# Order and queues of the first loads in a fused attention and feed-forward kernel

## The chip, the cores and the metric

The kernel runs on one core of a Trainium2 chip. The metric is the device time of one launch in microseconds (us). TensorE (PE) does the matmuls and the transposes, VectorE (DVE) and ScalarE (ACT) copy results out of PSUM and do the elementwise work, GpSimd (POOL) issues the loads that change float32 into bfloat16, and SyncE (SP) issues transfers that keep the type.

## What is computed

Attention inside blocks of 64 tokens, and a feed-forward layer with a product of two projections, without a nonlinearity:

```python
scores = scale * np.matmul(q_c, k_c.transpose(0, 1, 2, 4, 3))   # 8 batches, 8 heads, 9 blocks of 64, depth 64
scores = scores - np.max(scores, axis=-1, keepdims=True)
attn = np.exp(scores)
attn = attn / (np.sum(attn, axis=-1, keepdims=True) + 1e-09)
out = np.matmul(attn, v_c)
# heads side by side: x is 4608 x 512
a = x @ w1                 # 512 x 1024
b = x @ w2                 # 512 x 1024
h = a * b @ w3             # 1024 x 1024
return (h @ w_out)         # 1024 x 512
```

## The kernel before

The 4608 tokens are 36 groups of 128 (two blocks of 64 each) for the attention, and 9 tiles of four groups for the feed-forward layer. Since nothing stands between `w3` and `w_out`, the kernel multiplies them once, `w3o = w3 @ w_out`, and a tile then costs two projections (`add_tile`, line 491), one product on VectorE (line 500) and one matmul with `w3o` (line 522).

A group (`add_group`) takes q and k as bfloat16 from a `raw` buffer, of which there are six. Groups 0 to 11 are transposed on TensorE (line 337, with the identity `ident`), later ones by transfers of SyncE (line 341). Then come copies of k and of q's two halves, the scores (line 365), maximum, difference, exponential, sum and scaling, the transposes of the attention (line 396, or line 347 by transfer from group 16 on), the product with v (line 407) and a copy into `xt` (line 411). v is kept for one batch at a time in one of three buffers `vd0` to `vd2`, which are zeroed at the start: the first by VectorE, the other two by ScalarE (line 244). The loads of a batch of v are two transfers, one for each half of the partitions (line 273). Group 4 is the first that needs the second batch of v.

`w3o` is made in eight steps (`add_w3o`): a block of `w3` is transposed with `ident` (line 448), copied, and multiplied with `w_out` in two parts (line 459): with blocks 0 to 3 of `w_out` and with blocks 4 to 7. Blocks 4 to 7 come by one load of GpSimd (`load_wo`, line 301). Blocks 0 to 3 come in float32 by four transfers of SyncE (`stage_wo`, lines 306 to 321) into buffers of `o_sb`, and ScalarE casts them to bfloat16.

The order on every engine is written by a planner, `Plan.run`, which walks through the work with costs and keys, puts each operation on an engine, and emits them in the order in which it started them. What it assumes of transfers decides the order of the program and nothing else; on the chip the engines wait on semaphores. GpSimd's order is given: `LOADS` (lines 18 to 21) is the order of its first loads, with `('ident',)` where it makes the identity (`make_identity`, a memset and a select). `('w3', 7, 8)` is block 7 of `w3`, `('qk', 2)` q and k of group 2 (one transfer each, or two each where the group lies in two batches, as group 4 does), `('v', 0, 0, 2)` the first batch of v, `('w12', 0, 2)` four transfers with the first two eighths of `w1` and `w2`, `('wo', 4, 8)` blocks 4 to 7 of `w_out`. GpSimd's transfers use eight semaphores in turn, so that each issue waits for the landing of the transfer eight before it (`RING = 8`, line 67). `issue` is the time for which the planner thinks the issuing engine busy.

Ahead of the first attention product the kernel also puts fillers on TensorE (lines 575 to 585): matmuls of zeros, 14 at the start and then as many as fit into each gap that the planner sees.

Of the kernel before, what the change touches and what calls it, by code (L numbers as in the profile page):

```python
# [14 lines left out]

LOADS = [('qk', 0), ('w3', 7, 8), ('w3', 3, 4), ('qk', 1), ('w3', 0, 1), ('wo', 4, 8), ('w3', 1, 2), ('ident',),
         ('qk', 2), ('w3', 2, 3), ('w3', 5, 6), ('qk', 3), ('w3', 6, 7), ('qk', 5), ('qk', 4), ('v', 0, 0, 2), ('w3', 4,
         5), ('w12', 0, 2), ('qk', 6), ('w12', 4, 6), ('qk', 7), ('w12', 2, 4), ('w12', 6, 8), ('qk', 8), ('v', 1, 0, 2),  # L20
         ('qk', 9), ('qk', 10)]
TILES = [4] * 9
XT = 16
STAGED = 4
# [21 lines left out]
class Plan:  # L46
# [22 lines left out]
    def run(self):  # L69
        free = {e: 0.0 for e in ("PE", "ACT", "DVE", "POOL", "SP")}  # L70
        free["POOL"], free["SP"] = 1.2, 0.8
        todo = {e: [] for e in free}
        for i, o in enumerate(self.ops):
            o.place, o.left, o.since = i, len(set(map(id, o.after))), 0.0
        heirs = {}
        for o in self.ops:
            for d in {id(d): d for d in o.after}.values():
                heirs.setdefault(id(d), []).append(o)
            if not o.left:
                for e in o.engines:  # L80
                    todo[e].append(o)

        rings, flown, reach = {"POOL": [], "SP": []}, 2.2, {"POOL": 1.6, "SP": 1.3}
        left, now, order, ends = len(self.ops), 0.0, [], [0.8, 1.2]
        loads = [o for o in self.ops if "POOL" in o.engines]

        def ended(o):
            heapq.heappush(ends, o.end)
            for k in heirs.get(id(o), ()):
                k.left, k.since = k.left - 1, max(k.since, o.end)  # L90
                if not k.left:
                    for e in k.engines:
                        todo[e].append(k)

        def ready(o):
            if o.left or o.since > now:
                return False
            for n in o.takes:
                if n in self.turn and self.turn[n][len(self.taken[n])] is not o:
                    return False  # L100
                i = len(self.taken[n]) - self.bufs[n]
                if i >= 0 and any(u.end is None or u.end > now for u in self.taken[n][i].users[n]):
                    return False
            return True

        def heads(t):
            return [r[0] for r in rings.values() if r and r[0][0] <= t]

        while left or any(rings.values()):

            while flown < now:
                h = heads(flown)
                step = min([now - flown] + [x[1] * len(h) for x in h])
                step = min([step] + [r[0][0] - flown for r in rings.values() if r and r[0][0] > flown])
                flown = now if step >= now - flown else flown + step
                for x in h:
                    x[1] -= step / len(h)
                for r in rings.values():
                    if r and r[0] in h and r[0][1] < 1e-6:
                        o = r.pop(0)[2]  # L120
                        o.end = flown + o.lag
                        ended(o)
            for eng in free:
                if free[eng] > now or len(rings.get(eng, ())) >= self.RING:
                    continue
                pick = [o for o in (loads[:1] if eng == "POOL" else todo[eng]) if ready(o)]
                if not pick:
                    continue
                o = min(pick, key=lambda o: (o.key, o.place))
                for e in o.engines:  # L130
                    todo[e].remove(o)
                if eng == "POOL":
                    loads.pop(0)
                o.start, o.engine = now, eng
                cost = o.cost[o.engines.index(eng)] if isinstance(o.cost, tuple) else o.cost
                if o.issue:
                    free[eng] = now + o.issue
                    rings[eng].append([free[eng] + reach[eng], cost, o])
                else:
                    free[eng] = now + cost  # L140
                    o.end = now + cost + o.lag
                    ended(o)
                for n in o.takes:
                    self.taken[n].append(o)
                order.append(o)
                heapq.heappush(ends, free[eng])
                if o.issue:
                    heapq.heappush(ends, rings[eng][-1][0])
                left -= 1
            while ends and ends[0] <= now:  # L150
                heapq.heappop(ends)
            h = heads(now)
            after = ends[:1] + [flown + x[1] * len(h) for x in h]
            assert after or not left, "the plan is stuck"
            now = max(min(after, default=now), now + 1e-6)
        return order
# [3 lines left out]
def kernel(  # L160
# [19 lines left out]
    nc = tc.nc  # L180
# [6 lines left out]
    P = 128  # L187
# [18 lines left out]
    def sb(tag, shape, dt=bf, bufs=None):  # L206
        return work.tile(shape, dt, tag=tag, name=tag, bufs=bufs or BUFS[tag])
# [4 lines left out]
    ident = consts.tile([P, P], bf)  # L212
# [12 lines left out]
    plan = Plan(BUFS, ("qd", "kT", "kqT", "p_sc", "sd", "e", "an", "at", "p_av", "xt"))  # L225

    def copy(eng, o, i):
        if eng == "ACT":
            nc.scalar.copy(o, i)  # L229
        else:  # L230
            nc.vector.tensor_copy(o, i)  # L231
# [74 lines left out]
    def stage_wo(k0, k1):  # L306
        staged = []
        for ki in range(k0, k1):
            box = {}

            def emit(eng, ki=ki, box=box):
                box["t"] = sb("o_sb", [P, D_MODEL], f32)
                nc.sync.dma_start(box["t"][:], moe_w_out[ki * P:(ki + 1) * P])

            def cast(eng, ki=ki, box=box):
                copy(eng, wo_sb[:, ki, :], box["t"][:])

            o = plan.add("SP", 0.67, -2000 + ki, emit, takes=("o_sb",), lag=1.6, issue=0.1)
            staged.append(plan.add(("ACT", "DVE"), 0.6, -1500 + ki, cast, after=(o,), uses=[(o, "o_sb")]))
        wo_got.append(staged)  # L320
        wo_cut.append((k0, k1))
# [224 lines left out]
    if STAGED:  # L546
        stage_wo(0, STAGED)
    for what, *args in LOADS:
        if what == "ident":
# [68 lines left out]
```

## Time and profile before

| | |
|---|---|
| median of 3 runs | 254.52 us (252.12 to 254.99) |
| profiled execution, its own time | 252.69 us |
| its span | 250.9 us |
| TensorE busy | 239.3 us, 95% of the span |
| VectorE, ScalarE, GpSimd busy | 173.8, 146.3, 101.4 us |
| moved by transfers | 38.58 MB, mean 154 GB/s |
| idle time of TensorE ahead of the first transposes | 2.6 us |
| first transposes of q and k | 9.58 us from the start of the span |
| first matmul of line 491 | 39.07 us |
| first matmul that reads the second batch of v | 57.54 us, after 1.30 us idle |

All times in the profile are from the start of the span. "Landing" is the time from the start of an issue until the semaphore of the transfer is set. In the list of waits a line gives who waited, at which line, for whom, and then the total in us, how often, and the longest. In the chain of work a line gives the start, the length, and what took that time. q0 is the queue of GpSimd's transfers, q1 that of the transfers which SyncE issues.

### The profile page before, as it was taken

Reading aid. Unit: us, or ns where it says so; the run is one execution under the profiler, and the core shown is the slowest. Engines: PE = TensorE matmul, PEld = TensorE weight load, DVE = VectorE, ACT = ScalarE, POOL = GpSimd, SP = SyncE. Lnnn points to the kernel's source line nnn. Section 1 sums busy time; section 2 is a strip of 40 time slices with the busy share of each in tenths; the row PEclk is TensorE's granted clock in tenths of the full one; section 3 lists DMA queues with packets and bytes.
Section 4 is the critical chain, followed back from the end, with each engine's and each line's share of the span. In section 5 each row is a group of like instructions: output and inputs, shape, how many; then the busy total and the mean of one; then the engine's idle time right before and its main releaser. Section 6 shows DMA issues by size and latency. Waiting matters only on the chain.

```text
span 250.9 us, 4671 instructions
## 1 busy us (share of the span) xinstructions
PE 239.3 (95%) x1737; PEld 125.3 (50%) x1769; DVE 173.8 (69%) x315; ACT 146.3 (58%) x250; POOL 101.4 (40%) x127
## 2 busy tenths in 40 slices
PE   8599979998999999999999999999999999999994
PEld 2355755545555555545444545454454444444443
DVE  6176988976888889798778998887898842222310
ACT  8537686566867677667658466655666433433222
POOL 8656869887529764248326331720000000000000
PEclk9799999999999999999999999999999999999999
DMA  6999999999999999999999999999979994121114
GB/s 157 191 195 185 139 176 178 180 147 144 139 120 150 147 155 158 157 134 153 141 131 156 157 139 157 135 154 149 160 119 353 295 340 138 42 84 43 42 44 167
DMA packets 160454, 38.58 MB, mean 154 GB/s; under 512 B 149424, under 2 KB 154416, under 8 KB 160432
## 3 DMA queue, kind: packets, MB, share of 16 engines
q0 software_dynamic: 118160, 18.88, 114.5%
q1 hardware_dynamic: 42272, 19.41, 41.9%
q8 instruction: 14, 0.23, 0.4%
q14 instruction: 8, 0.07, 0.1%
HBM read 38.80 MB, written 9.44 MB: 192 GB/s over the span
## 4 chain that ended last, share of the span: by engine, by line
PE 76%; DMA 16%; POOL 3%; issue 3%; DVE 1%; ACT 1%; POOLq 0%
PE ffn L491 41%; PE ffn L522 23%; DMA vd<-in_v_dram 7%; DMA at<-an 4%; PE p_av L407 3%; PE p_sc L365 3%; DMA raw<-in_q_dram 3%; DMA raw<-in_k_dram 2%; PE ffn L459 2%; PE ffn L337 1%; PE p_av L585 1%; POOL raw L267 1%; POOL vd L273 1%; PE ffn L396 1%; PE ffn L448 1%
## 5 line engine op out<-in xcount | busy, mean ns | idle before, releaser
L491 PE MATMUL ffn<-xt,w_sb 128*128 128x512 bf16 x555 | 131.6, 379 | 1.1
L491 PEld LDWEIGHTS <-w_sb 128*128 128x128 bf16 x576 | 53.9, 98 | 58.3
L500 DVE TENSOR_TENSOR abT<-a_sb,ffn 128x512 bf16<-128x512 f32 x72 | 48.7, 679 | 36.6 <-PE ffn L491 34.8
L522 PE MATMUL ffn<-w3o_sb,abT 128*128 128x512 bf16 (+2 forms) x298 | 66.8, 368 | 0.4
L229 ACT COPY a_sb<-ffn 128x512 f32<-128x512 f32 x72 | 42.0, 583 | 34.1 <-PE ffn L491 33.5
L267 POOL DMA_DIRECT2D raw<-in_q_dram x40 | 34.3, 860 | 33.6 <-DMA kqT<-raw 13.6
L522 PEld LDWEIGHTS <-abT 128*128 128x128 bf16 x304 | 28.1, 98 | 29.6
L267 POOL DMA_DIRECT2D raw<-in_k_dram x40 | 34.1, 852 | 19.3 <-DMA vd<-in_v_dram 9.6
L373 DVE TENSOR_REDUCE nm<-p_sc 128x8 f32<-128x512 f32 x36 | 24.3, 676 | 6.5 <-PE p_sc L365 6.5
L229 ACT COPY o_sb<-ffn 128x512 f32<-128x512 f32 (+2 forms) x20 | 10.8, 542 | 29.4 <-PE ffn L522 29.3
L385 DVE TENSOR_REDUCE ss<-e 128x8 f32<-128x520 bf16 x36 | 24.8, 688 | 3.5 <-ACT e L381 3.3
L381 ACT ACTIVATE e<-sd 128x512 bf16<-128x512 f32 x36 | 22.8, 634 | 3.9 <-DVE sd L377 3.5
L377 DVE TENSOR_TENSOR sd<-p_sc,nm 128x512 f32<-128x512 f32 x36 | 24.5, 681 | 0.5
L391 DVE TENSOR_TENSOR an<-e,rs 128x512 bf16<-128x512 bf16 x36 | 24.6, 684 | 0.2
L229 ACT COPY qd<-kqT 64x512 bf16<-64x512 bf16 x37 | 22.7, 614 | 2.7 <-DMA kqT<-raw 2.4
L229 ACT CAST xt<-p_av 128x512 bf16<-128x512 f32 x27 | 15.8, 586 | 10.1 <-PE p_av L407 9.9
L273 POOL DMA_DIRECT2D vd<-in_v_dram x16 | 18.5, 1162 | 5.7 <-PE ffn L491 2.8
L407 PEld LDWEIGHTS <-vd 128*128 128x128 bf16 x288 | 13.0, 98 | 10.4 <-issue 1.5
L407 PE MATMUL p_av<-at,vd 128*128 128x64 bf16 x288 | 14.4, 193 | 2.4 <-DMA vd<-in_v_dram 1.7
L459 PE MATMUL ffn<-wo_sb,w3t 128*128 128x512 bf16 x60 | 15.6, 379 | 0.6 <-DVE w3t L231 0.4
L365 PEld LDWEIGHTS <-qd 128*128 128x128 bf16 x288 | 12.6, 99 | 5.4 <-DVE qd L231 0.4
L285 POOL DMA_DIRECT2D w_sb<-in_moe_w_dram x16 | 9.9, 629 | 2.2 <-DMA vd<-in_v_dram 0.8
(44 smaller groups left out, 150.9 us busy)
## 6 DMA issues: line engine op xcount, KB each, us to landing
out_dram<-o_sb SPq DMA_DIRECT2D x23, 256.0 KB, 2.4
vd<-in_v_dram POOLq DMA_DIRECT2D x16, 288.0 KB, 9.7
raw<-in_q_dram POOLq DMA_DIRECT2D x32, 128.0 KB, 9.3
raw<-in_k_dram POOLq DMA_DIRECT2D x32, 128.0 KB, 9.3
w_sb<-in_moe_w_dram POOLq DMA_DIRECT2D x8, 256.0 KB, 8.8
w_sb<-in_moe_w_dram POOLq DMA_DIRECT2D x16, 128.0 KB, 5.7
out_dram<-w_sb SPq DMA_DIRECT2D x8, 256.0 KB, 2.5
o_sb<-in_moe_w_out_dram SPq DMA_DIRECT2D x4, 256.0 KB, 3.9
```

Source lines behind the costliest of these rows:

```text
L229: nc.scalar.copy(o, i)
L267: nc.gpsimd.dma_start(box["t"][r, w], src[b, :, c * C:(c + n) * C, :].rearrange("h p d -> p h d"))
L273: nc.gpsimd.dma_start(vds[b % len(vds)][halves[t], 2 * y0:2 * y1, :, t * D:(t + 1) * D].rearrange("p m c d -> p (m c) d"), v[b, NM * t + 2 ...
L373: nc.vector.tensor_reduce(nm[:, :, 0], flat(box["sc"]), axis=AX.X, op=ALU.max)
L377: nc.vector.tensor_sub(sd[:], flat(box["sc"]), box["nm"].to_broadcast([P, 8, C]))
L381: nc.scalar.activation(e[:, :, :C], box["sd"][:], ACT.Exp, scale=scale)
L385: nc.vector.reduce_sum(ss[:], box["e"][:], axis=AX.X)
L391: nc.vector.tensor_mul(an[:], box["e"][:, :, :C], box["rs"].to_broadcast([P, 8, C]))
L407: nc.tensor.matmul(t[:, m, cc, :], vds[b % len(vds)][:, m, c, :], box["at"][:, 2 * cc + y, u * C:(u + 1) * C], start=True, stop=True)
L491: nc.tensor.matmul(t[:, :w], wt[:, ki, j * P:(j + 1) * P], x[:, ki, :], start=(ki == 0), stop=(ki == KO - 1))
L500: nc.vector.tensor_mul(box["abT"][:, j, :w], box["as", j][:, :w], box["b", j][:, :w])
L522: nc.tensor.matmul(t[:, :x1 - x0], box["abT"][:, ki, tk * P:(tk + 1) * P], w3o_sb[:, ki, x0:x1], start=(ki == 0), stop=(ki == FO - 1))
```

## The change

The identity is made ahead of all loads instead of after the ninth transfer. The first 25 loads stand in another order: among them the blocks of `w3`, and q and k of group 5, which now come after the first v and after the last two blocks of `w3`. Blocks 1 and 3 of `w_out` are issued by ScalarE and not by SyncE, in its program after the zeroing of the second v buffer and ahead of that of the third. The planner takes 0.23 instead of 0.1 us for these issues, and lets a load of GpSimd hold one of its eight places for 1.3 us more; both move other operations on the engines, but only in the first 60 us of the program.

```diff
-LOADS = [('qk', 0), ('w3', 7, 8), ('w3', 3, 4), ('qk', 1), ('w3', 0, 1), ('wo', 4, 8), ('w3', 1, 2), ('ident',),
-         ('qk', 2), ('w3', 2, 3), ('w3', 5, 6), ('qk', 3), ('w3', 6, 7), ('qk', 5), ('qk', 4), ('v', 0, 0, 2), ('w3', 4,
-         5), ('w12', 0, 2), ('qk', 6), ('w12', 4, 6), ('qk', 7), ('w12', 2, 4), ('w12', 6, 8), ('qk', 8), ('v', 1, 0, 2),
-         ('qk', 9), ('qk', 10)]
+LOADS = [('ident',), ('qk', 0), ('w3', 4, 5), ('qk', 1), ('wo', 4, 8), ('w3', 0, 1), ('qk', 2), ('w3', 3, 4), ('w3',
+         6, 7), ('w3', 7, 8), ('w3', 1, 2), ('qk', 3), ('qk', 4), ('v', 0, 0, 2), ('w3', 5, 6), ('w3', 2, 3), ('qk',
+         5), ('w12', 0, 2), ('qk', 6), ('w12', 2, 4), ('qk', 7), ('w12', 4, 6), ('w12', 6, 8), ('qk', 8), ('v', 1, 0,
+         2), ('qk', 9), ('qk', 10)]
...
-        left, now, order, ends = len(self.ops), 0.0, [], [0.8, 1.2]
+        landed, left, now, order, ends = [], len(self.ops), 0.0, [], [0.8, 1.2]
...
                         o.end = flown + o.lag
+                        if o.engine == "POOL":
+                            landed.append(flown + 1.3)
+                            heapq.heappush(ends, landed[-1])
                         ended(o)
...
-                if free[eng] > now or len(rings.get(eng, ())) >= self.RING:
+                if free[eng] > now or len(rings.get(eng, ())) + (eng == "POOL" and sum(x > now for x in landed)) >= self.RING:
...
-                nc.sync.dma_start(box["t"][:], moe_w_out[ki * P:(ki + 1) * P])
+                (nc.sync, nc.scalar)[ki % 2].dma_start(box["t"][:], moe_w_out[ki * P:(ki + 1) * P])
...
-            o = plan.add("SP", 0.67, -2000 + ki, emit, takes=("o_sb",), lag=1.6, issue=0.1)
+            o = plan.add("SP", 0.67, -2000 + ki, emit, takes=("o_sb",), lag=1.6, issue=0.23)
```

## The prediction

> **What bounds the kernel now.** I read the table of busy time by slices first, then the waits of TensorE, then the chain of work that ended last, then the loads' own queue. The page says that TensorE is nearly always at work:
>
> ```profile
> PE 239.3 (95%) x1737; PEld 125.3 (50%) x1769; DVE 173.8 (69%) x315; ACT 146.3 (58%) x250; POOL 101.4 (40%) x127
> ...
> PE   8599979998999999999999999999999999999994
> ```
>
> So a change to the first loads can win only in the first slices, where the digits fall below 9. The waits of TensorE over the whole span (total us, times, longest us) name the places:
>
> ```profile
> PE ffn L337 <- POOL ident masks.py:199: 2.6, 1, 2.6
> PE p_av L407 <- DMA vd<-in_v_dram: 1.7, 2, 1.3
> PE p_av L585 <- DVE nought L237: 1.2, 1, 1.2
> PE p_av L407 <- ACT xt L229: 0.5, 1, 0.5
> ```
>
> Two matter: 2.6 us at the first transposes, put down to the identity, and 1.3 us in the middle, put down to the second load of v. The chain in order of time (start, us) shows that the second is the one that decides:
>
> ```profile
> 1.25 6.87 DMA raw<-in_q_dram
> ...
> 9.24 0.30 POOL ident masks.py:199
> 9.58 0.80 PE ffn L337 x8
> ...
> 47.13 1.11 POOL vd L273
> 48.24 9.24 DMA vd<-in_v_dram
> 57.54 0.29 PE p_av L407 x4
> ```
>
> Whatever TensorE gains ahead of 57.54 us it loses again there, as long as that load does not land sooner. The timeline of TensorE around it, with the idle time in brackets:
>
> ```profile
> 39.07 1.03 PE L491 MATMUL ffn<-xt,w_sb 128*128 128x512 bf16 x4
> ...
> 55.96 0.28 PE L407 MATMUL p_av<-at,vd 128*128 128x64 bf16 x4
> 57.54 0.29 PE L407 MATMUL p_av<-at,vd 128*128 128x64 bf16 x4 [1.30 <-DMA vd<-in_v_dram]
> ```
>
> TensorE is ready at 56.24 and goes on at 57.54. From there to the end of the span are 250.9 - 57.5 = 193.4 us, with one wait of 0.2 us (on a transposed `at`) in them. The load itself is the 49th that GpSimd issues. GpSimd has at most eight transfers open, and the transfers wait in their queue: landing takes 5.8 to 10.7 us from issue in the first 28 us. The queue by windows of two us (26 to 28, 48 to 50, 52 to 54) holds 2250, 2050 and 2100 packets, so it never runs dry on the way to that load. The next lines are the two queues in the windows 2 to 3, 4 to 5, 5 to 6 and 7 to 8 us (packets, MB, share of 16 engines):
>
> ```profile
> q1 hardware_dynamic: 149, 0.29, 91.8%
> ...
> q1 hardware_dynamic: 87, 0.15, 43.2%
> q0 software_dynamic: 160, 0.02, 31.8%
> ...
> q0 software_dynamic: 292, 0.04, 57.8%
> q1 hardware_dynamic: 56, 0.10, 40.4%
> ...
> q0 software_dynamic: 741, 0.15, 172.4%
> q1 hardware_dynamic: 29, 0.04, 13.7%
> ```
>
> q1 holds SyncE's four blocks of `w_out`, q0 GpSimd's loads. The reader is to see that q0 begins only after 4 us (its first packet is at 4.3), 3 us after GpSimd's first issue at 1.25, and is slow while q1 still has packets.
>
> **The change part by part.** The sum is made against the profiled execution (span 250.9, its own time 252.69, so 1.8 us lie around the span). It is 1.8 us under the median of the three runs, 254.52, which range from 252.12 to 254.99; I carry the difference over to the median.
>
> 1. What stays. Built, the changed kernel gives TensorE the same matmuls ahead of the first one that reads the second v buffer: 72 transposes of q and k, 64 of w3, 64 matmuls of line 459 and 64 of line 491, and so on, with 26 fillers instead of 25. After it the order is the same to the end. GpSimd issues the same 48 transfers ahead of the second half of that v load, and from the 26th on in the same order. So the new time is the landing of that load, or TensorE's arrival if that is later, plus 193.4 us.
>
> 2. The identity goes ahead of all loads. In the trace it takes GpSimd from 8.94 to 9.48, 0.54 us. At the head it delays the first issue, 1.25, by that: +0.54 on q0's start. Where it was, the queue had eight transfers in hand, so taking it away there gives q0 nothing. Bounds: 0, if q0 would wait anyhow for q1 (43% of the engines at 4 to 5 us, 160 packets of q0); and +0.68, if it also meets what makes GpSimd's first issue 1.01 us long where later ones take 0.87. I take 0.54.
>
> 3. Two of SyncE's four blocks go to ScalarE. SyncE's issues take 0.42 us each, 0.74 to 2.56. ScalarE's two stand behind its table load and its first zeroing of a v buffer, which end at 2.03 and about 4.09 us, and ahead of the second. If they wait for the zeroing, they are issued at 4.1 to 4.9 and all of their 288 packets (half of 576) run beside q0; if only for the table load, they start about as before. Today 87 + 56 + 65 + 29 = 237 packets of q1 run beside q0. At 149 a us (the window 2 to 3, where q1 is alone) one costs q0 0.0067 us. So late issue costs (288 - 237) x 0.0067 = +0.35, and early issue, with q0 starting 0.54 later, when some 50 more packets of q1 are through, gives -0.35. But late issue also leaves the engines to q0 alone for its first half us, where the trace has them shared. I take -0.2, between them.
>
> The Trainium skill, DMA: Bandwidth & Descriptors, section "Issuing engines are not separate DMA queues", says that transfers from several engines end up on the same 16 DMA engines, and that issuing from several at once saves only the issue time on the sequencer. By it the split would give nothing beyond the 0.84 us of SyncE's last two issues, on an engine with nothing else to do then, and the sum would be +0.54 alone. The trace agrees as far as it goes: q0 moves at 292 packets a us while q1 holds 40% of the engines, and at 741 when it holds 14%.
>
> 4. ScalarE pays for the two issues: 2 x 0.42 = 0.84 us before its second zeroing (2.06) and its four casts (0.62 each, the last at 7.91 today). ScalarE is idle for 1.89 us before its first copy of k at 10.41, which covers the 0.84. If a late block lands 5.8 us after issue, the longest of today's four, the last cast ends at 4.9 + 5.8 + 0.6 = 11.3, and the copy of k, its scores and the fillers behind them come 0.9 us later. That is still inside the 1.3 us of wait at 56.24, so it costs 0, and 0.9 if the cover were gone. The filler more (0.22) is covered likewise.
>
> 5. The first transposes need k landed as well as the identity. k0 was issued at 2.26 and took 6.7 us, so it landed at 8.96; the weight load of TensorE starts at 9.03. Without the wait on the identity the transposes could start about 0.5 us sooner, less the shift of q0. In the trace the granted clock then falls to 0.50 from 10 to 13 us, after an idle stretch of 2.62 us; eight transposes take 0.8 to 0.9 us instead of 0.45. Half of 3.3 us, 1.6, could come back if the idle stretch gets short enough. All of it ends in the same wait, so I cost it at 0.
>
> The Trainium skill, TensorE: Matmul & The Clock Gate, Part 1, says that the clock is judged in free-running windows of about 3.4 us and falls after an idle one. By it a shorter gap might keep the clock up, or the windows might fall otherwise from run to run. The trace agrees in size, about 3.3 us at half clock. The sum would be the same: 1.6 us sooner at a load that is not there.
>
> 6. The order of the first loads. Ahead of the 26th load both orders move the same: all of w3, half of w_out, q and k of groups 0 to 5, the first v. The first v comes 3 places sooner; q and k of group 5 move from places 17 and 18 to 24 and 25, where a block of w3 stood last. That block let GpSimd go on at 35.41 after 0.23 us, so it landed near 35.1. Group 5 then lands near 35.1 plus the shift, and behind it TensorE has its transposes (0.45), 12 matmuls of line 459 (2.59), one set of scores and one of attention transposes (0.48): line 491 starts at about 38.9 plus the shift, against 39.07 now. From there it is the same 17.2 us to the wait: arrival 56.1 plus the shift. The load still comes last, by about 1.4 us.
>
> Sum: 0.54 - 0.2 = +0.3 us on the landing, so 57.8, and a span of 251.2. On the median that is 254.52 + 0.3 = 254.8.
>
> **The rivals.**
>
> A, the queue gets ahead. The first two loads, 2048 small packets, landed at 8.96, some 4.7 us after q0 began; at 26 to 28 us the same number goes through in 1.8. Of the 2.9 lost, 237 x 0.0067 = 1.6 are q1's packets; 1.3 are not explained. If half of q1 out of the way gives these back and the identity costs nothing, the load lands 1.3 us sooner, at 56.2, which is also where TensorE arrives: 253.2. For it: q0 more than doubles its rate as q1 runs out. Against it: q0 is still at 741 a us without much of q1, and ScalarE's blocks bring q1 back.
>
> B, slower: TensorE takes the place of the load as the last to arrive, because q and k of group 5 now come so late. Everything from line 491 on stands behind their transposes in TensorE's order. It decides from the point where line 491 starts after 40.6 (57.8 - 17.2), that is, when group 5 lands later than 37.1 instead of 35.4. Whole loads of q or k issued from 9 to 33 us took 7.2 to 10.7 us, so 2 us of spread exist. Landing 2.8 us late would make it +1.1 over the forecast: 255.9. Against it: places 24 and 25 carry the same bytes before them as now.
>
> C, the queue is simply later by all of it: 0.68 + 0.35 = +1.0, 255.5. For it: nothing in the trace shows that q0 waits for q1 before it starts. Against it: ScalarE's issues may go out while the zeroing runs.
>
> That the change does nothing to the time is my forecast itself: it removes a wait that another wait hides.
>
> **How the numbers follow.** The forecast 0.5, with its own range of -0.3 to +0.9 about the median: 254.2 to 255.4. A 0.2, B 0.15, C 0.15. The three runs of one kernel spread by 1.4 us to either side of their middle, so the range goes from 252.0 (A less 1.2) to 257.0 (B and C plus 1.3). Over or under 1%, 2.5 us, is about what a measurement of this kernel can tell from no change. Faster by more needs A and a low median, 0.18; slower by more needs B or C and a high one, 0.17; the rest is 0.65.
>
> **What would show it.** Right: TensorE's wait on the identity is gone, the wait on the second v load is still there and of 1 to 2 us, its matmul starts at 57.5 to 58.4, and 193.4 us follow. Step 2 is wrong if q0's first packets come no later than now; step 3, if q0 moves over 600 packets a us at 5 to 6 us; step 6, if the wait on v is gone and one on q or k of group 5, or on w3, stands ahead of line 491. The prediction fails if the load lands 2 us sooner or later, or if the 193.4 us are not kept.

## The result, and the profile after

| | before | after |
|---|---|---|
| median of 20 runs | 251.98 us (250.06 to 254.99) | 253.58 us (251.52 to 254.84, one disturbed run of 317.55 left out of the ratio) |
| ratio | | 1.0066, 95% interval 1.0043 to 1.0090 |
| profiled execution | 252.69 us, span 250.9 | 252.99 us, span 251.2 |

The change makes the kernel 0.66% slower, 1.6 us. That is a small loss, clear of the measurement's noise and inside 1%. The median of before over 20 runs is 251.98; the 254.52 that the prediction started from was the middle of three runs, two of which happened to lie high, and the profiled execution of before is 0.7 us over the median while that of after is 0.6 under its own. So the two profiled executions, 0.3 us apart, are not the measured difference, and single traces are read below for places and not for totals.

The page of after, busy time and the row of slices of TensorE:

```profile
PE 240.1 (96%) x1770; PEld 122.6 (49%) x1770; DVE 174.6 (70%) x314; ACT 148.8 (59%) x251; POOL 101.3 (40%) x127
...
PE   7698999989999999999999999999999999999995
```

The waits of TensorE over the span (total us, times, longest us):

```profile
PE ffn L340 <- DMA raw<-in_k_dram: 2.7, 2, 2.1
PE p_av L588 <- DVE nought L240: 1.2, 1, 1.2
PE p_sc L368 <- DVE qd L234: 1.0, 2, 0.7
PE p_av L410 <- DMA vd<-in_v_dram: 0.8, 1, 0.8
PE p_av L410 <- DMA at<-an: 0.5, 1, 0.5
PE ffn L399 <- DVE an L394: 0.4, 1, 0.4
PE p_av L410 <- ACT wo_sb L232: 0.4, 1, 0.4
```

The wait on the identity is gone, the wait on v is 0.8 instead of 1.3, and among the new ones are 0.5 us on transposed attention (`at`) and 0.4 put down to `wo_sb`, which was done long before, so that what really ended this wait is not named by the profile. The timeline of TensorE at the first transposes and at the second batch of v:

```profile
7.82 0.62 PE L340 MATMUL ffn<-ident,raw 128*128 128x128 bf16 x8 [2.08 <-DMA raw<-in_k_dram]
...
56.12 0.29 PE L410 MATMUL p_av<-at,vd 128*128 128x64 bf16 x4 [0.83 <-DMA vd<-in_v_dram]
```

Those were 9.58 and 57.54. So in this execution the changed kernel is 1.4 us ahead at 57 us, and yet its span is 0.3 longer: 251.2 - 56.1 = 195.1 us follow the matmul on the second v, where 193.4 did. Adding up, from TensorE's timeline, how much later each group of matmuls starts than its length allows gives the place ("lost time" from here on): 9.27 us lost before 60 us (10.90 in the kernel before), 2.45 from 90 to 175 us (0.77 before). It is a sum over many small gaps, good to a few tenths of a us.

What differs in between is on GpSimd. First the kernel before, then after (start, length, instruction, idle time before it):

```profile
67.87 0.87 POOL L267 DMA_DIRECT2D raw<-in_q_dram  x1 [1.87 <-PE p_av L407]
69.26 0.87 POOL L267 DMA_DIRECT2D raw<-in_k_dram  x1 [0.52 <-DMA vd<-in_v_dram]
74.51 0.88 POOL L267 DMA_DIRECT2D raw<-in_q_dram  x1 [4.37 <-DMA kqT<-raw]
75.38 0.88 POOL L267 DMA_DIRECT2D raw<-in_k_dram  x1
76.24 2.32 POOL L273 DMA_DIRECT2D vd<-in_v_dram  x2
```

```profile
66.59 0.88 POOL L270 DMA_DIRECT2D raw<-in_q_dram  x1 [2.15 <-PE p_av L410]
67.50 0.88 POOL L270 DMA_DIRECT2D raw<-in_k_dram  x1
68.36 0.88 POOL L270 DMA_DIRECT2D raw<-in_q_dram  x1
69.23 0.89 POOL L270 DMA_DIRECT2D raw<-in_k_dram  x1
70.09 2.33 POOL L276 DMA_DIRECT2D vd<-in_v_dram  x2
...
80.18 0.88 POOL L270 DMA_DIRECT2D raw<-in_q_dram  x1 [4.25 <-DMA kqT<-raw]
```

The third line of each is the load of group 16's q. Before, it waits 4.37 us for SyncE's transposes of group 12 (`kqT<-raw`), since it is to overwrite the `raw` buffer which they read. After, it has another buffer and does not wait; group 17's load, behind the batch of v, got group 12's buffer, and comes to it when the transposes are done. GpSimd's pause comes with the load of group 19 at 80.18, for the transposes of group 13; by then groups 16 to 18 and the batch of v are issued. Which of the six `raw` buffers a load gets, here called the hand-out, is settled by a pool when the program is built, and the change gave another hand-out. By what rule the pool chooses is not shown: in run e1 below, moving the identity alone gives yet another one. On GpSimd and SyncE the instructions after 60 us stand in the same order in both kernels; only the buffer, and with it a semaphore to wait for, differs.

What that does to the transfers shows in the window 72 to 86 us (packets by size; then packets, MB, share by queue; then issues with their median us to landing), before and after:

```profile
DMA packets 12854, 2.03 MB, mean 145 GB/s; under 512 B 12853, under 2 KB 12853, under 8 KB 12853
...
raw<-in_q_dram POOLq DMA_DIRECT2D x5, 128.0 KB, 9.0
vd<-in_v_dram POOLq DMA_DIRECT2D x2, 288.0 KB, 8.7
raw<-in_k_dram POOLq DMA_DIRECT2D x4, 128.0 KB, 9.9
kqT<-raw SPq DMA_TRANSPOSE x4, 7.3
```

```profile
DMA packets 11153, 1.82 MB, mean 130 GB/s; under 512 B 11152, under 2 KB 11152, under 8 KB 11152
...
raw<-in_q_dram POOLq DMA_DIRECT2D x4, 128.0 KB, 14.6
raw<-in_k_dram POOLq DMA_DIRECT2D x3, 128.0 KB, 17.1
vd<-in_v_dram POOLq DMA_DIRECT2D x1, 288.0 KB, 16.0
kqT<-raw SPq DMA_TRANSPOSE x3, 11.1
```

Without the pause, GpSimd's loads of groups 16 to 18 and a batch of v stand in the queues beside SyncE's transposes of groups 13 to 15. The same engines move 1700 packets fewer in 14 us, a load takes 15 to 17 us to land instead of 9 to 10, and a transpose of SyncE (`kqT<-raw`) 11.1 instead of 7.3. The packets of the transposes of those three groups run from 73.1 to 85.7 us after the change, 12.6 us, against 74.0 to 82.0, 8.0 us, before. From group 19 on each load has the buffer of the group six before it, in both kernels, so behind the first twelve groups the hand-outs differ for groups 16 to 18 alone.

### The profile page after: what moved, and what is told of

Its sections match the earlier page's. It is cut to its first block, busy times and chain, and to the rows that moved or that the text cites. A ratio compares the mean times of both kernels' runs of the same rounds, so it can differ in the third digit from the quotient of the medians.

```text
span 251.2 us, 4708 instructions
## 1 busy us (share of the span) xinstructions
PE 240.1 (96%) x1770; PEld 122.6 (49%) x1770; DVE 174.6 (70%) x314; ACT 148.8 (59%) x251; POOL 101.3 (40%) x127
## 4 chain that ended last, share of the span: by engine, by line
PE 52%; DMA 36%; POOL 5%; issue 2%; ACT 1%; DVE 1%; SPq 1%; POOLq 0%; ACTq 0%
PE ffn L494 26%; PE ffn L525 19%; DMA raw<-in_k_dram 13%; DMA vd<-in_v_dram 9%; DMA raw<-in_q_dram 5%; POOL raw L270 4%; DMA at<-an 4%; DMA w_sb<-in_moe_w_dram 3%; DMA kqT<-raw 3%; PE p_av L410 2%; PE ffn L462 2%; PE p_sc L368 1%; PE ffn L340 1%; SPq L344 1%; PE ffn L399 0%
## 5 line engine op out<-in xcount | busy, mean ns | idle before, releaser
L494 PE MATMUL ffn<-xt,w_sb 128*128 128x512 bf16 x576 | 134.3, 379 | 0.0
L525 PE MATMUL ffn<-w3o_sb,abT 128*128 128x512 bf16 (+2 forms) x304 | 67.6, 368 | 0.0
L232 ACT COPY o_sb<-ffn 128x512 f32<-128x512 f32 (+2 forms) x20 | 10.9, 543 | 28.9 <-PE ffn L525 28.8
L232 ACT CAST xt<-p_av 128x512 bf16<-128x512 f32 x24 | 14.0, 585 | 7.5 <-PE p_av L410 7.4
L462 PE MATMUL ffn<-wo_sb,w3t 128*128 128x512 bf16 x64 | 15.8, 379 | 0.0
L368 PEld LDWEIGHTS <-qd 128*128 128x128 bf16 x288 | 12.1, 98 | 7.2 <-DVE qd L234 1.6
L234 DVE CAST xt<-p_av 128x512 bf16<-128x512 f32 x12 | 8.3, 691 | 5.5 <-PE p_av L410 5.4
```

The costliest lines, as they stand in the source:

```text
L462: nc.tensor.matmul(box["wp"][:], box["t"][:, ki, :], wo_sb[:, ki, :], start=(ki == wo_cut[0][0]), stop=(ki == wo_cut[-1][1] - 1))
L494: nc.tensor.matmul(t[:, :w], wt[:, ki, j * P:(j + 1) * P], x[:, ki, :], start=(ki == 0), stop=(ki == KO - 1))
L525: nc.tensor.matmul(t[:, :x1 - x0], box["abT"][:, ki, tk * P:(tk + 1) * P], w3o_sb[:, ki, x0:x1], start=(ki == 0), stop=(ki == FO - 1))
```

## The experiments

The first eight runs test where the time is lost and which part of the change loses it. The last four test the buffers. All ratios are to the kernel before, run on the same chip in turn.

**One part alone.** Run e1 emits the kernel before in its own order, with the identity moved to the head and nothing else:

```diff
-        for o in plan.run():
+        for o in sorted(plan.run(), key=lambda o: o is not made_ident):
```

> The kernel before with one part of the change: the identity made ahead of the loads; every other engine keeps its order. Theory M (the time is set in the middle, between 90 and 170 us, where GpSimd's loads and SyncE's transposes share the DMA engines, and what is won ahead of the second v load is lost there): first transposes 0.3 to 0.5 us sooner, start of the matmul on the second v within 0.5 us of before, span within 0.6 us of before. Rival L (the new order of the first loads costs the time, the other parts nothing): the same as before, ratio 0.998 to 1.002. Rival I (the identity at the head makes every load later): the second v lands 0.5 us later or more, ratio 1.002 to 1.004.

Run e2 changes only who issues blocks 1 and 3 of `w_out`:

```diff
-                nc.sync.dma_start(box["t"][:], moe_w_out[ki * P:(ki + 1) * P])
+                (nc.sync, nc.scalar)[ki % 2].dma_start(box["t"][:], moe_w_out[ki * P:(ki + 1) * P])
```

> The kernel before with one part of the change: blocks 1 and 3 of w_out issued by ScalarE; every order stays. Theory M: the first packets of q0 run faster, the matmul on the second v starts up to 1 us sooner, and that is lost between 90 and 170 us: span within 0.6 us of before. Rival L: no change of the time, ratio 0.998 to 1.002. Rival S (the split carries the gain at the start): the matmul on the second v 1 us sooner, and the span 1 us shorter, ratio 0.996.

Run e3 is the changed kernel with that line as it was before, so it has the identity and the new order of loads.

> The changed kernel with all four blocks of w_out issued by SyncE again: new order of loads and identity at the head, orders on the engines as in the changed kernel. Theory M: as the changed kernel within 0.6 us, with the lost time between 90 and 170 us over 1.5 us. Rival L: ratio 1.004 to 1.009, all of the change's loss, wherever it is lost. Rival S: slower than the changed kernel by 1 us.

Run e4 is the changed kernel again, on the chip of e1 to e3.

> The changed kernel once more, beside the three others and with another profile. Theory M: the matmul on the second v starts ahead of 57.0 us again and TensorE loses over 1.5 us between 90 and 170 us. A theory that the first profile was an exception, and that the second v usually lands later than before: matmul on the second v after 58 us, under 1 us lost between 90 and 170. Ratio 1.004 to 1.009 either way.

| run | median us | ratio, 95% interval | lost time 90 to 175 us (one trace) |
|---|---|---|---|
| e1, identity alone | 252.73 | 1.0051 (1.0027 to 1.0074) | 2.61 |
| e2, ScalarE's issues alone | 250.96 | 0.9981 (0.9956 to 1.0006) | 2.93 |
| e3, identity and loads | 252.79 | 1.0051 (1.0027 to 1.0075) | 0.78 |
| e4, the changed kernel again | 254.08 | 1.0102 (1.0066 to 1.0139) | 2.63 |

Moving the identity alone brings a loss of 0.5%, the new order of loads adds nothing to it that can be told, and the issues from ScalarE cost nothing by themselves. Whether they cost something on top of the other parts is not settled here: e4 lies 0.5% over e3, with intervals that just overlap, and the same kernel was at 1.0066 in the result. Several expectations failed. In e1 the matmul on the second v started at 55.47, 2.1 us sooner, more than any of its theories had, and the kernel lost more than they had. In e3 the lost time is under the 1.5 us that theory M asked for. e4's trace is as theory M had it (56.12 and 2.63). The lost time of single traces does not sort the kernels: e2 loses most and is the fastest, e3 loses little and is slow. It depends on how early TensorE arrives, too: in the 14 traces of this study the stretch ahead of 60 us lost from 8.1 to 12.1 us, for one and the same kernel 9.2 and 10.9.

**Less work for the transfers.** If the early gain were given back because SyncE's transposes in the middle limit the pace, it should come out where those of the attention are taken away. e5 is the kernel before with the attention transposed on TensorE in all groups, e6 the same with the identity at the head, e7 the changed kernel with the same:

```diff
-QK_BY_DMA, A_BY_DMA = set(range(12, 36)), set(range(16, 36))
+QK_BY_DMA, A_BY_DMA = set(range(12, 36)), set()
```

> The kernel before with the transposes of the attention of groups 16 to 35 on TensorE instead of by transfers of SyncE. TensorE gets 20 x 0.23 = 4.6 us more work, the DMA engines 20 transposes less. Theory M: no wait on a transposed attention is left between 90 and 170 us; span about 250 + 4.6 = 254.6. It is the base for the next two.

> The run before this one with the identity made ahead of the loads, all else in the same order. Theory M (the identity's place costs time only through the middle, where loads and transposes share the DMA engines): the gain ahead of the second v, 1 to 2 us, is now kept, so 1 to 2 us less than the run before this one. Rival I (the identity at the head costs by itself): 1.3 us more than the run before this one, as with the kernel before.

> The changed kernel with the attention transposed on TensorE throughout. Theory M: 1 to 1.5 us less than the kernel before with the same (the gain ahead of the second v load that the profile of the changed kernel shows). Rival I: 1.5 us more.

Run e8 is the kernel before again, on that chip.

> The kernel before once more, for a second profile of it. Theory M: the matmul on the second v starts at 55 to 57.7 us, and TensorE's lost time between 90 and 170 us makes up what is missing to about 11 us over the whole span. Rival I: the first loads of q and k land sooner than in the run with the identity at the head, by 0.5 us or more.

e5 took 255.32 us (1.0139, 1.0087 to 1.0191), e6 257.53 (1.0225, 1.0175 to 1.0275), e7 257.85 (1.0242, 1.0187 to 1.0297), e8 251.90 (1.0001, 0.9958 to 1.0043). The loss did not go away with the transposes of the attention: by medians e6 is 2.2 us over e5 and e7 2.5 us over it, more than the 1.6 of the change itself. So theory M, by which the transposes of the attention in the middle eat an early gain, fell. e8's trace has the matmul on the second v at 55.84, inside theory M's range, but loses next to nothing from 90 to 175 us (0.3), where the theory had it make up about 11 us in all; its first load of k lands at 8.13 us, against 8.07 in e1 and 8.93 in e6, so that rival I's sign comes out both ways. What after, e1, e3, e4, e6 and e7 have in common, and before, e2, e5 and e8 have not, is the hand-out of `raw`: the former let GpSimd run on where the others pause for group 12's transposes.

**The buffers alone.** Three kernels name the six buffers by hand, with no operation moved on any engine. In e9 the changed kernel gets the hand-out of the kernel before; in e10 the kernel before gets them in turn, which is where the waits of e1 are; e11 is the control, before with its own hand-out (the same from group 12 on; the loads of groups 10 and 11 have each other's buffer). In the cut below the first `return` is that of e9 and e11, the second that of e10:

```diff
+    raw_t = [wpool.tile([P, 2, H, D], bf, tag=f"raw{i}", name=f"raw{i}") for i in range(6)]
+
+    def raw_at(g):
+        return ([0, 1, 2, 3, 4, 5, 0, 1, 2, 3, 4, 5, 0, 1, 2, 3] + [0, 4, 5, 1, 2, 3] * 4)[g]   # e9, e11
+        return g % 6   # e10
...
-                        box["t"] = sb("raw", [P, 2, H, D])
+                        box["t"] = raw_t[raw_at(g)]
```

> The changed kernel with six raw buffers named by hand, handed out as the kernel before has them: the load of group 16 takes the buffer of group 12 (and waits for SyncE's transposes of group 12), 17 that of 10, 18 that of 11. The order on every engine is that of the changed kernel. Theory S (the loss after 60 us comes from which buffer the loads of groups 16 to 18 get: with the changed kernel's hand-out GpSimd does not pause near 68 us, its loads run beside the transposes of groups 13 to 15, and those take about 4 us instead of 2): ratio 0.994 to 1.001, GpSimd pauses for some 5 us between 66 and 74 us again, bursts of transposes of about 2 us, TensorE's lost time between 90 and 175 us under 0.9 us (the changed kernel: 2.5 to 2.6). Rival I (the early identity or the early ScalarE issues cost by themselves, whatever the buffers): ratio 1.004 to 1.009 as for the changed kernel, lost time still over 2 us.

> The kernel before with six raw buffers handed out in turn, so that the load of group 18, not that of 16, takes the buffer of group 12, as it does where the identity alone is moved. Nothing else is changed: order of the first loads, identity and issuing engines are those of the kernel before. Theory S: ratio 1.003 to 1.008 with no identity moved, GpSimd issues on through 68 to 73 us, the transposes of groups 13 to 15 take about 4 us each, lost time between 90 and 175 us over 2 us. Rival I: ratio 0.998 to 1.002, lost time as in the kernel before (0.3 to 0.8 us).

> Control: the kernel before, its own hand-out of the raw buffers written by hand as in the two others, so only the way in which the buffers are named differs. Both theories: ratio 0.998 to 1.002. If it is off by more than that, the naming by hand itself costs, and the two others are to be read against this one.

| run | median us | ratio, 95% interval | packets, 72 to 86 us | transposes of groups 13 to 15 take |
|---|---|---|---|---|
| e9, changed kernel, buffers of before | 251.71 | 0.9988 (0.9959 to 1.0017) | 12744 | 74.6 to 82.5, 7.9 us |
| e10, before, buffers in turn | 253.15 | 1.0049 (1.0014 to 1.0085) | 11811 | 75.1 to 87.1, 12.0 us |
| e11, before, its own by hand | 251.34 | 0.9967 (0.9934 to 1.0001) | 12971 | 75.5 to 83.1, 7.6 us |

GpSimd in e9, which has the pause again, and in e10, which has lost it:

```profile
68.72 0.87 POOL L274 DMA_DIRECT2D raw<-in_q_dram  x1 [2.01 <-PE p_av L414]
69.59 0.88 POOL L274 DMA_DIRECT2D raw<-in_k_dram  x1
75.11 0.87 POOL L274 DMA_DIRECT2D raw<-in_q_dram  x1 [4.64 <-DMA kqT<-raw]
75.98 0.88 POOL L274 DMA_DIRECT2D raw<-in_k_dram  x1
76.84 2.33 POOL L280 DMA_DIRECT2D vd<-in_v_dram  x2
```

```profile
69.82 0.87 POOL L271 DMA_DIRECT2D raw<-in_k_dram  x1 [0.77 <-DMA raw<-in_q_dram]
70.68 0.88 POOL L271 DMA_DIRECT2D raw<-in_q_dram  x1
71.55 0.90 POOL L271 DMA_DIRECT2D raw<-in_k_dram  x1
72.42 2.33 POOL L277 DMA_DIRECT2D vd<-in_v_dram  x2
```

And the transfers of the window 72 to 86 us in e9 and e10:

```profile
raw<-in_q_dram POOLq DMA_DIRECT2D x5, 128.0 KB, 9.4
vd<-in_v_dram POOLq DMA_DIRECT2D x2, 288.0 KB, 8.8
raw<-in_k_dram POOLq DMA_DIRECT2D x4, 128.0 KB, 9.3
kqT<-raw SPq DMA_TRANSPOSE x4, 7.5
```

```profile
vd<-in_v_dram POOLq DMA_DIRECT2D x2, 288.0 KB, 14.0
raw<-in_k_dram POOLq DMA_DIRECT2D x4, 128.0 KB, 15.8
raw<-in_q_dram POOLq DMA_DIRECT2D x4, 128.0 KB, 15.7
kqT<-raw SPq DMA_TRANSPOSE x4, 9.9
```

The kernel before, untouched but for its buffers, becomes as slow as with the identity moved (1.0049 against 1.0051; against its control 253.15 / 251.34 = 1.0072). The changed kernel, untouched but for its buffers, is level with before. So the loss is the hand-out of the buffers, and the rival, that the early identity or the early issues cost the 0.4 to 0.9% by themselves, is out: with the buffers held as they were, all the parts of the change together are worth -0.1%, with an interval that holds zero. The control itself came out at 0.9967, under the 0.998 to 1.002 expected for it, though its interval just reaches 1. Read against it, as its expectation asks, e9 is at 251.71 / 251.34 = 1.0015, so that a cost of one or two tenths of a percent for the rest of the change is not ruled out. Added up in the same way, the time lost from 90 to 175 us is about 2.5 us in e10, as expected, and 0.8 in e11. In e9 it is 1.51 us, where under 0.9 was expected. Its profiled execution is the slowest of its twelve runs, 253.85 us against a median of 251.71, and 1.2 of the 1.51 is one wait put down to `wo_sb`, as in after. e11's profiled execution, 253.87, is also far above its median.

**A longer pause.** e12 asks whether more of the pause is better: the changed kernel, with the loads of groups 16 to 19 each in the buffer of group 12 to 15, so that each waits for transposes.

```diff
+        return ([0, 1, 2, 3, 4, 5, 0, 1, 2, 3, 4, 5, 0, 1, 2, 3] + [0, 1, 2, 3, 4, 5] * 4)[g]
```

> The changed kernel with the six raw buffers named by hand so that the loads of groups 16, 17, 18 and 19 take the buffers of groups 12, 13, 14 and 15, each of which waits for SyncE's transposes of that group: GpSimd pauses four times instead of once. The order on every engine is that of the changed kernel. It asks whether the pause is worth having because it keeps loads away from the transposes. If the gain of the kernel before comes from that alone: the four transposes near 68 to 82 us take about 2 us each, TensorE's lost time between 90 and 175 us is under 0.9 us, ratio 0.993 to 1.001, at or under the run with the single pause (0.9988). If a longer pause makes the loads themselves late: transposes of about 2 us there all the same, but TensorE waits later for loads (v, w1, w2) or for transposes of later groups, and the ratio is 1.003 or more. Rival I (the early identity costs by itself): 1.004 to 1.009 with transposes that do not take 4 us.

It took 252.18 us, ratio 1.0028 (0.9990 to 1.0065): between the two outcomes, and its interval overlaps both that of e9 and that of the changed kernel. The trace has 12863 packets from 72 to 86 us, the transposes of groups 13 to 15 from 73.4 to 82.9 us (9.5 us), and 0.68 us lost from 90 to 175. So the crowd of transfers is smaller, and no gain over the single pause is seen; whether the longer pause costs something elsewhere is not settled. No run beats the kernel before beyond its interval; e2 and e11 come nearest, at 0.9981 and 0.9967.

## Why the prediction was right or wrong

The total was right for a reason that was not among its reasons, and so by luck. The range 252.0 to 257.0 holds 253.58, and "within 1%" was the likeliest case. Behind it a base 2.5 us too high and a loss that the sum does not have nearly cancel, and by its own signs the mechanism failed: the matmul on the second v did not start at 57.5 to 58.4 but at 56.12, and the 193.4 us were not kept.

The base: 254.52 was taken as the median and the 1.8 us over the profiled execution carried along. Over 20 runs the median is 251.98, below that execution. Against the profiled execution's own 252.69, the forecast of +0.3 would have been 253.0; measured, median against median, the change is +1.6.

Step 1 is the one that failed: "After it the order is the same to the end", and so "plus 193.4 us". The order is the same; the waits are not. The buffers of `raw` were handed out otherwise, GpSimd's pause of some 4.3 us moved from ahead of a batch of v and the loads of three groups to behind them, and 195.1 us followed in the trace of after. Over the traces, 192.9 to 194.1 us follow that matmul in before, e8, e9, e11 and e12, and 195.1 to 195.3 in after, e1, e4 and e10; e2 (195.5) and e3 (193.4) do not fit. With the attention transposed on TensorE it is 197.5 in e5, and 199.4 and 199.0 in e6 and e7. With no order changed, the hand-out is worth 0.5% in e10 (0.7% against its control), and e9 gives back the loss (1.0066 to 0.9988). The prediction named GpSimd's waits only for places in its queue, and never asked what each load waits for besides.

Step 2 took +0.54 for the identity at the head. GpSimd's first issue went from 1.25 to 1.44, +0.19: it had idled 0.81 us before that issue anyway, and the memset starts inside that time, at 0.74. The nearer bound was 0. The step's own sign misleads in the trace of after, where q0's first packet comes at 4.77 us and not at 4.33. In e1, e3 and e6, with the identity at the head and all four blocks on SyncE, it comes at 4.18 to 4.20, and in the five kernels with the identity in its old place and the blocks on SyncE at 4.10 to 4.33. In all six with ScalarE's issues, e2 among them, it comes at 4.70 to 4.97. So the early identity does not delay q0's start at all; the split does.

Step 3 gave two cases for ScalarE's issues, late behind the zeroing or early. They were early, 1.20 to 2.06, while ScalarE was still loading its table:

```profile
0.73 1.28 ACT L247 ACT_TABLE_LOAD   x1 [0.73 <-PEq L605]
1.20 0.86 ACTq L316 DMA_DIRECT2D o_sb<-in_moe_w_out_dram  x2
2.03 4.12 ACT L247 COPY vd<-nought 128x2304 f32<-128x2304 f32 x2
```

In ScalarE's program the two stand behind the first zeroing, which ran from 2.03 on; so they did not wait for it: the case priced at -0.35 is the one that came about, where -0.2, between the two, was taken. By its own test, q0 over 600 packets a us at 5 to 6 us, the step was wrong: it moved 1117 there, against 292 before.

```profile
q0 software_dynamic: 1117, 0.14, 221.5%
```

Over all traces it is 894 to 1117 with ScalarE's issues and 292 to 485 without, and the first load of k lands at 7.4 to 8.0 us with them and at 8.1 to 9.4 without. So q0 starts later and is ahead soon after; the early case had a later start too, but put it down to the identity. That this is worth nothing to be measured, e2 shows (0.9981, interval to 1.0006). The section "Issuing engines are not separate DMA queues" of the Trainium skill, DMA: Bandwidth & Descriptors, which has issuing from several engines save issue time alone, agrees with that as far as the kernel's time goes.

Steps 4 and 6 cost nothing, as forecast: e2, which holds step 4, is not slower; the first matmul of line 491 (494 after) starts at 38.24 instead of 39.07, and e3 with the new order of loads is no slower than e1 without it. Rival B, group 5 too late, did not happen.

Step 5: the first transposes came 1.76 us sooner (7.82), and the clock's row, which the prediction expected might stay up, does: the mean granted clock is 1.000 after and 0.993 before. The Trainium skill, TensorE: Matmul & The Clock Gate, Part 1, has the window of idleness at some 3.4 us; the idle stretch went from 2.62 to 2.08 us here, so the trace does not show which condition kept it up. The length of the stretch alone does not decide: e2 has 1.89 us of it, and the clock is at 0.50 from 10 to 12 us all the same, while e1 has 2.19 and stays at 1.00.

The gate at 57.54 us was itself a sample. The load of v is waited for in most traces, but the matmul behind it starts at 57.54 and at 55.84 in two executions of the kernel before, at 58.72 in the control and at 56.12 in both of the changed one. Rival A, v landing sooner, looks true in the first pair of traces (56.12 against its 56.2) and is not shown by the set: the gain at the first load of k, which all six traces with ScalarE's issues have, is not to be found at the second v, where these six start the matmul at 54.7 to 58.1 and the other eight at 55.5 to 58.7. The prediction's price of 0.3 us there was far under the spread of its own quantity.

What stays open: how the hand-out turns into the time lost. The crowd of loads and transposes comes with it: in the window 72 to 86 us the median landing of SyncE's transposes is 7.2 to 8.4 us in the seven traces with the pause and 9.9 to 11.1 in the seven without, and that of the loads of k 8.7 to 11.6 and 15.8 to 17.1. But no run changes the crowd and not the hand-out, why both go slower side by side is not shown, and the packets sort the kernels less sharply: e3 (12561 packets, 11.5 us for the transposes) and e2 (12224, 10.8) lie close to each other there and 0.7% apart in time.

## What to carry to other kernels

Compare what each instruction waits for, and not only the order of the instructions: where a pool hands out buffers, moving an early operation can give a load much later another buffer, and move a wait past a large transfer. A wait of a load's issuer is not always a loss; the kernel that waits 4.4 us ahead of these loads is the faster one here. And where a step is worth tenths of a us, take a second execution of the same kernel before building on an instant in the first: the one used here moved by 1.7 us.

## What the runs showed of the hardware

Transposes by transfer and GpSimd's loads go slower side by side: three groups of transposes take 7.6 to 8.0 us behind the pause in before, e9 and e11 and 12.0 to 12.6 us beside the loads in after and e10, and the median landing of a 128 KB load goes from 9 to 10 us to 15 to 17. With a shorter pause (2.50 us, e2) they take 10.8 us, so the pause does not keep them apart in every case.

ScalarE's two transfers were issued from 1.20 us on, during a table load that began at 0.73 and ended at 2.01, and ahead of a copy that stands before them in its program.

Moving two of four early transfers from SyncE to ScalarE made the first packets of GpSimd's queue come later (4.70 to 4.97 us instead of 4.10 to 4.33) and its first load of k land sooner (7.4 to 8.0 instead of 8.1 to 9.4), in every trace.
